# Attention values in half precision by casting transfers of the GpSimd queue, on one core

## The chip, the cores and the metric

The kernel runs on one core of a Trainium2 chip. The metric is the device time of one execution in microseconds (us). A core has five engines that run at the same time, each with a queue of instructions that it takes strictly in order: TensorE (PE, matmuls; PEld are its weight loads), VectorE (DVE), ScalarE (ACT), GpSimd (POOL) and SyncE (SP, which here issues transfers). Transfers between memory and the on-chip buffers run on 16 DMA engines.

## The reference, cut to what matters

A block-causal attention over 8 batches with 8 heads, 576 positions and a head size of 64 (blocks of 64 positions) is followed by a gated linear unit whose gate is a causal convolution over 5 positions.

```python
scores = scale * np.matmul(q, k.transpose(0, 1, 3, 2))       # q, k, v: (8, 8, 576, 64) fp32
scores = np.where(block_i >= block_j, scores, -1e9)
attn = np.exp(scores - scores.max(-1, keepdims=True)); attn /= attn.sum(-1, keepdims=True)
x = np.matmul(attn, v).transpose(0, 2, 1, 3).reshape(8, 576, 512)
gate = sigmoid(sum(conv_w[k] * xp[:, k:k + 576, :] for k in range(5)))
out = (gate * (x @ w_val)) @ w_out                           # fp32
```

## The kernel before

The 64 heads are worked as 32 pairs; pair p is two heads of batch p // 4. The first 512 key positions of a pair are four blocks of 128, the last 64 positions (the tail) are handled per batch. Nothing is left to a scheduler: a text `PLAN` lists words `name/arguments/engine/bank`, and the kernel emits one operation for each word in that order. The order of the words of one engine is the order of that engine's queue. The engine letters are P (TensorE), V (VectorE), A (ScalarE), G (GpSimd) and S (SyncE).

The words that matter here:

- `lq`, `lk` (line 265) load q and k of two pairs, one half each, in fp32 into `qks`; `cd` (line 253) casts them to fp16 on GpSimd or VectorE; `Tt` transposes them on TensorE and `Te` moves the result to `qkT`.
- `S(p, t)` makes the scores of pair p in three parts, `E(p, t)` (line 449, ACT) writes their exponentials to `pts`, six buffers used in turn. `mka` and `mkb` (lines 494 and 499, GpSimd) then zero the masked blocks of `pts`.
- `lv(p, h)` (line 281) loads the values of head h of pair p, 512 rows of 64 fp32 numbers, from SyncE into the staging tiles `vs`, five buffers in turn. `cv(p)` (line 253) casts both heads of pair p from `vs` into `v16s`, seven buffers in turn whose rows are 65 wide: 64 values and a column of ones that `pv` (line 333) writes once. `cv` runs 24 times on GpSimd and 8 times on VectorE.
- `lvt` and `cvt` do the same for the tail, in `vts` and `v16t`.
- `A(p)` on TensorE multiplies the exponentials by `v16s`; the column of ones gives the sums of the softmax. `AT(b)` does it for the tail queries of batch b and reads all four pairs of the batch again. `Nr` and `Nm` (lines 523 and 528, VectorE) normalize, `X` and `Xe` transpose into `xt`.
- `C`, `CS`, `V`, `Ve`, `O`, `Oe`, `Od` are the convolution as matmuls, the gate, the two products and the output. `lcv`, `ccv`, `CW` and `CWe` load, cast, transpose and spread the convolution's weights at the start. `w0` are matmuls on zeros.

The opening (pairs 0 to 3 in halves: `Tth`, `Teh`, `Sh`, `Eh`) comes before the steady part, in which score work of later pairs is mixed with the gated unit of earlier batches. The words after the last attention pair are the output's.

Of the kernel before, what the change touches and what calls it, by code (L numbers as in the profile page):

```python
# [30 lines left out]
E/5.1/A S/6.1/P/6+7 mkb/4/G Nr/2/V AT/0/P/0 Nm/2/V E/6.1/A lk/4.1/S Xe/3/V S/5.0/P/4+5 NTr/0/V
X/2/P/2+3 lv/6.0/S w0/1.128.0/P/1 E/5.0/A Xe/2/V mka/6/G S/7.2/P/6+7 NTm/0/V cwv/1/G S/6.2/P/2+3
E/7.2/A C/0/P/0+1+4+5 lv/6.1/S cwv/0/V E/6.2/A cwo/0/V V/0.3/P/6 CS/0.1/A lq/5.0/S cwo/1/G V/0.2/P/7
CS/0.0/A Ve/0.3/V S/7.1/P/4+5 V/0.0/P/2 Ve/0.2/V E/7.1/A lq/5.1/S cd/4.0/G W//P/0+1+6+7 Ve/0.0/V
lv/5.1/S S/7.0/P/4+5 We/1/A We/0/V V/0.1/P/3 lv/5.0/S mkb/6/G cv/4/G lv/7.1/S E/7.0/A Tt/4.0/P/6+7
Ve/0.1/V lv/7.0/S XT/0/P/2 cd/4.1/G A/4/P/0+1 Te/4.0/A lvt/1/S O/0.0/P/3 Nr/4/V Nm/4/V lk/5.0/S
cv/6/G XTe/0/A SL/1/P/6+7 Oe/0.0/V Tt/4.1/P/4+5 mka/5/G lq/6.0/S EL/1/A mka/7/G A/6/P/0+1 mkb/7/G
Te/4.1/A mkb/5/G O/0.2/P/6 lk/5.1/S cd/5.0/V lq/6.1/S Nr/6/V Tt/5.0/P/4+5 Nm/6/V Oe/0.2/A X/4/P/4+5
lv/8.0/S S/9.2/P/2+3 cv/5/G Te/5.0/V S/8.2/P/6+7 E/9.2/A A/5/P/0+1 E/8.2/A Xe/4/V lv/9.1/S
S/8.0/P/2+3 Nr/5/V cv/7/V S/9.0/P/4+5 lv/8.1/S E/8.0/A cvt/1/G Nm/5/V A/7/P/6+7 lv/10.0/S E/9.0/A  # L40
S/9.1/P/0+1 lv/9.0/S Nr/7/V AT/1/P/2 Nm/7/V lv/10.1/S E/9.1/A S/8.1/P/4+5 lk/6.1/S X/5/P/6+7
cd/5.1/G X/7/P/6+7 X/6/P/6+7 O/0.1/P/3 E/8.1/A Xe/7/V lk/6.0/S Xe/6/V mkb/9/G Xe/5/V Tt/5.1/P/0+1
cd/6.0/G Oe/0.1/A NTr/1/V C/1/P/4+5+6+7 NTm/1/V Te/5.1/A mkb/8/G lv/11.1/S mka/8/G Tt/6.0/P/2+3
CS/1.0/A Od/0.0/S V/1.2/P/0 cv/8/V lv/11.0/S Te/6.0/V CS/1.1/A lk/7.1/S S/11.1/P/4+5 V/1.0/P/1
cv/9/G lvt/2/S E/11.1/A Ve/1.2/V cv/10/G lq/7.1/S S/10.0/P/2+3 Ve/1.0/V A/8/P/6+7 mka/9/G E/10.0/A
lk/7.0/S S/10.2/P/0+1 Nr/8/V S/10.1/P/4+5 lq/7.0/S Nm/8/V E/10.2/A V/1.1/P/2 lv/12.1/S cd/6.1/V
E/10.1/A S/11.2/P/6+7 lv/14.0/S Ve/1.1/V S/11.0/P/0+1 V/1.3/P/3 lvt/3/S E/11.2/A cv/11/V mkb/10/G
A/9/P/4+5 mka/10/G Ve/1.3/V E/11.0/A mkb/11/G Tt/6.1/P/6+7 Nr/9/V A/10/P/2+3 Nm/9/V Te/6.1/A
# [36 lines left out]
E/22.2/A Od/1.2/S S/23.1/P/4+5 Ve/5.1/V lv/26.0/S Tt/12.0/P/0+1 E/23.1/A S/23.2/P/6+7 mkb/22/G
# [34 lines left out]
def kernel(  # L120
# [123 lines left out]
    def rot(tiles, i):  # L244
        return tiles[i % len(tiles)]
# [519 lines left out]
```

## Time and profile before

| what | value |
|---|---|
| time, median of 2 runs | 179.12 us (178.89 to 179.35) |
| the profiled execution | 177.31 us, span 175.5 us |
| PE busy | 165.6 us, 94% |
| ACT busy | 144.8 us, 82% |
| DVE busy | 121.6 us, 69% |
| POOL busy | 70.9 us, 40% |
| transfers | 40.38 MB, 53,694 packets |
| mean granted TensorE clock | 0.968 |

The span runs from the first to the last instruction of the profiled execution; the time around it is that of the whole execution. A busy share is an average over stages that have different limits: an engine with 40% can still be the one that others wait for in a stage. Each group of instructions is named by its line, engine, operation and tiles; a helper such as the copy at line 253 stands for several words of the plan, which the tile names tell apart.

### The profile page before, as it was taken

How to read it: one execution, taken by the hardware profiler on the slowest of the kernel's cores; microseconds unless marked ns; L12 is line 12 of the kernel's file. 1: busy time of each engine (PE TensorE's matmuls, PEld its weight loads, DVE VectorE, ACT ScalarE, POOL GpSimd, SP SyncE). 2: the span in 40 equal slices, each digit the busy share in tenths (PEclk: the TensorE clock that was granted, in tenths of full speed). 3: DMA queues.
4: the chain of work that ended last, by engine and by line, in shares of the span. 5: the costliest groups of instructions: out<-in, count | busy, mean ns of one | idle time of the engine just before them, and what ended most of it. 6: DMA issues, size and time to landing. Idle time of an engine off the chain costs nothing.

```text
span 175.5 us, 8114 instructions
## 1 busy us (share of the span) xinstructions
PE 165.6 (94%) x3498; PEld 99.6 (57%) x3498; DVE 121.6 (69%) x247; ACT 144.8 (82%) x179; POOL 70.9 (40%) x146
## 2 busy tenths in 40 slices
PE   6799899899999899899999999999999999999991
PEld 1456566456756465567556755665556665664540
DVE  2547998588769683999756998976698685545420
ACT  3799999889999699789889679988898878954562
POOL 5121875772552631486533643174546440100000
PEclk9855999999999999999999999999999999999998
DMA  4999899999999779998999969999987022103175
GB/s 141 306 364 280 234 241 392 327 232 252 238 301 262 132 185 287 334 292 241 311 327 246 304 197 259 290 302 222 322 253 213 4 97 86 63 4 120 38 296 209
DMA packets 53694, 40.38 MB, mean 230 GB/s; under 512 B 39701, under 2 KB 39957, under 8 KB 53658
## 3 DMA queue, kind: packets, MB, share of 16 engines
q1 hardware_dynamic: 53514, 39.74, 78.7%
q8 instruction: 27, 0.44, 1.1%
q10 hardware_dynamic: 144, 0.13, 0.2%
q14 instruction: 9, 0.07, 0.1%
HBM read 30.42 MB, written 9.44 MB: 227 GB/s over the span
## 4 chain that ended last, share of the span: by engine, by line
PE 80%; ACT 9%; DVE 3%; issue 3%; DMA 2%; SPq 0%; DVEq 0%; ACTq 0%
PE PS L144 72%; PE PS L148 8%; ACT pt L449 7%; DMA qs<-in_q_dram 2%; DVE gv L658 1%; ACT qkT L251 1%; DVE x L528 1%; DVE qkT L253 1%; DVE xt L253 0%; ACT q L251 0%; SPq L265 0%; ACT osb L251 0%; DVE rc L523 0%; ACT pt L488 0%; ACT late L251 0%
## 5 line engine op out<-in xcount | busy, mean ns | idle before, releaser
L449 ACT ACTIVATE pt<-PS 128x1024 f16<-128x1024 f32 (+1 forms) x102 | 93.8, 988 | 10.4 <-PE PS L144 8.8
L144 PE MATMUL PS<-qkT 64*128 64x64 f16 (+4 forms) x512 | 39.7, 257 | 2.3 <-issue 0.8
L144 PE MATMUL PS<-w_out,gv 128*128 128x512 f16 (+1 forms) x148 | 35.7, 374 | 0.2 <-DVE x L528 0.2
L144 PE MATMUL PS<-xt,w_val 128*128 128x464 f16 x160 | 35.7, 360 | 0.0
L658 DVE SCALAR_TENSOR_TENSOR gv<-th,PS 128x112 f16<-128x112 f32 (+4 forms) x64 | 26.2, 450 | 12.3 <-PE PS L144 6.0
L253 DVE COPY qkT<-PS 128x1152 f16<-128x1152 f16 (+1 forms) x22 | 29.1, 1326 | 8.1 <-PE PS L148 4.0
L144 PEld LDWEIGHTS <-pt 128*128 128x128 f16 (+1 forms) x960 | 27.9, 102 | 6.5 <-issue 1.8
L144 PE MATMUL PS<-v,pt 128*128 128x65 f16 (+1 forms) x896 | 31.1, 194 | 0.2 <-issue 0.2
L144 PEld LDWEIGHTS <-qkT 64*128 64x128 f16 x512 | 17.7, 96 | 18.6 <-issue 14.2
L640 ACT ACTIVATE th<-PS 128x928 f32<-128x928 f32 x20 | 17.8, 941 | 7.2 <-PE PS L144 7.1
L528 DVE TENSOR_TENSOR x<-PS,rc 128x512 f16<-128x512 f32 x32 | 22.1, 691 | 1.0
L144 PEld LDWEIGHTS <-w_val 128*128 128x128 f16 x160 | 13.9, 97 | 15.2 <-issue 3.6
L499 POOL MEMSET pt<- 64x256 f16 x32 | 10.9, 345 | 27.7 <-ACT pt L449 27.3
L144 PEld LDWEIGHTS <-gv 128*128 128x128 f16 x148 | 12.6, 97 | 13.5 <-issue 2.2
L253 POOL CAST k<-ks 128x1152 f16<-128x1152 f32 x12 | 13.8, 1148 | 11.9 <-DMA ks<-in_k_dram 6.0
L253 POOL CAST q<-qs 128x1152 f16<-128x1152 f32 x11 | 12.6, 1147 | 12.9 <-PE PS L144 6.1
L253 POOL CAST v<-vs 128x512 f16<-128x512 f32 x24 | 14.6, 618 | 6.7 <-DMA vs<-in_v_dram 5.1
L494 POOL MEMSET pt<- 64x256 f16 x32 | 10.0, 313 | 17.3 <-ACT pt L449 16.5
L253 DVE COPY xt<-PS 128x512 f16<-128x512 f16 (+1 forms) x30 | 11.6, 397 | 4.5 <-ACT th L640 2.3
L251 ACT COPY qkT<-PS 128x1152 f16<-128x1152 f16 (+1 forms) x16 | 14.2, 908 | 0.4 <-PE PS L148 0.4
L144 PE MATMUL PS<-xt,DG 32*32 32x464 f16 x800 | 13.0, 358 | 0.8 <-issue 0.7
L253 DVE COPY osb<-PS 128x512 f32<-128x512 f32 x17 | 11.6, 687 | 2.4 <-PE PS L144 1.7
(57 smaller groups left out, 135.3 us busy)
## 6 DMA issues: line engine op xcount, KB each, us to landing
ks<-in_k_dram SPq DMA_DIRECT2D x32, 288.0 KB, 5.0
qs<-in_q_dram SPq DMA_DIRECT2D x32, 288.0 KB, 5.5
out_dram<-osb SPq DMA_DIRECT2D x35, 256.0 KB, 4.3
vs<-in_v_dram SPq DMA_DIRECT2D x64, 128.0 KB, 5.1
vts<-in_v_dram SPq DMA_DIRECT2D x8, 128.0 KB, 5.0
osb<-in_moe_w_out_dram SPq DMA_DIRECT2D x2, 512.0 KB, 4.6
gv<-in_moe_w_val_dram SPq DMA_DIRECT2D x2, 512.0 KB, 5.7
out_dram<-late SPq DMA_DIRECT2D x1, 128.0 KB, 2.0
```

The costliest lines, as they stand in the source:

```text
L144: made.append(nc.tensor.matmul(out=out, lhsT=lhsT, rhs=rhs, start=start, stop=stop, skip_group_check=True))
L148: made.append(nc.tensor.transpose(out=out, in_=in_, identity=identity))
L251: i = nc.scalar.copy(out=out, in_=in_)
L253: i = (nc.vector if eng == "V" else nc.gpsimd).tensor_copy(out=out, in_=in_)
L449: made.append(nc.scalar.activation(out=o, in_=r, func=AF.Exp, bias=0.0, scale=0.125))
L494: nc.gpsimd.memset(rot(pts, p)[64:128, 0:2, 0:1024].rearrange("p h (t s) -> p h t s", t=2)[:, :, :, 0:64], 0.0)
L499: nc.gpsimd.memset(rot(pts, p)[64:128, 0:2, 640:1408].rearrange("p h (t s) -> p h t s", t=2)[:, :, :, 0:64], 0.0)
L528: made.append(nc.vector.tensor_tensor(out=rot(x16, p)[0:128].rearrange("p i h d -> p h i d"), in0=r[:, :, :, 0:64], in1=rot(rcs, p)[0:128] ...
L640: made.append(nc.scalar.activation(out=rot(ths, n)[0:128, 2 * i:2 * i + 2], in_=both(take("C", n, i))[:, :, 0:RUN], func=AF.Tanh, bias=0.0 ...
L658: made.append(nc.vector.scalar_tensor_tensor(out=gv[0:128, x, a - 4 * i:e - 4 * i], in0=rot(ths, n)[0:128, x, a - o:e - o], scalar=1.0, in ...
```

## The change

`lv` writes its rows straight into `v16s`, as fp16, and is issued from the GpSimd queue, which casts in the transfer. The staging tiles `vs` and all 32 `cv` are removed. All other words of the plan keep their order.

```diff
-    vs = consts(5, [128, 4, 2, 64], fp32, "vs")
...
-    DMA = {"S": nc.sync, "A": nc.scalar}
+    DMA = {"S": nc.sync, "A": nc.scalar, "G": nc.gpsimd}
...
     def lv(p, h, eng="S", bank=None):
         b, g = divmod(p, 4)
         DMA[eng].dma_start(
-            out=rot(vs, p)[0:128, 0:4, h, 0:64],
+            out=rot(v16s, p)[0:128, 0:4, h, 0:64],
             in_=v[b, 2 * g + h, 0:512, 0:64].rearrange("(c p) d -> p c d", p=128))
...
-    @op
-    def cv(p, eng, bank=None):
-        copy(eng, rot(v16s, p)[0:128, 0:4, 0:2, 0:64], rot(vs, p)[0:128])
```

In `PLAN` the 64 words `lv/p.h/S` and the 32 words `cv/p` are gone. The words `lv/0.0/G lv/0.1/G lv/1.0/G lv/1.1/G` stand between `pv` and `pt` at the start. The other pairs stand two words together, nearly always where a `cv` stood; some of the places, in order:

| pair loaded | stands where | pair loaded | stands where |
|---|---|---|---|
| 2 | `cv/0` | 9 | `cv/7` (VectorE) |
| 3 | `cv/1` | 12 | `cv/10` |
| 5 | `cv/3` | 21 | `cv/19` |
| 4 | `cv/2` | 24 | `cv/22` |
| 6 | `cv/4` | 27 | `cv/25` |
| 8 | `cv/6` | 31 | `cv/29` |
| 7 | `cv/5` | 30 | `cv/28` |

```diff
-E/2.0/A w0/1.128.0/P/4 lv/2.0/S cv/0/G Te/2.0/V S/3.2/P/4+5 E/2.2/A lv/2.1/S Tt/3.0/P/2+3 mkb/1/G
-mka/2/G mkb/0/G lwo/0/S Te/3.0/V E/3.2/A cv/1/G S/3.0/P/6+7 A/0/P/0+1 mka/1/G E/3.0/A S/4.1/P/4+5
+E/2.0/A w0/1.128.0/P/4 lv/2.0/G lv/2.1/G Te/2.0/V S/3.2/P/4+5 E/2.2/A Tt/3.0/P/2+3 mkb/1/G mka/2/G
+mkb/0/G lwo/0/S Te/3.0/V E/3.2/A lv/3.0/G lv/3.1/G S/3.0/P/6+7 A/0/P/0+1 mka/1/G E/3.0/A S/4.1/P/4+5
```

More of the change, by code (lines that the diff above doesn't have):

```diff
@@ L31 @@
[L31 to L48, printed above, removed]
@@ new lines @@
+lv/4.1/G S/6.0/P/0+1 Nr/3/V S/5.1/P/4+5 Nm/3/V cvt/0/G E/6.0/A A/2/P/2+3 px//G Xe/1/V mka/4/G
+X/3/P/2+3 E/5.1/A S/6.1/P/6+7 mkb/4/G Nr/2/V AT/0/P/0 Nm/2/V E/6.1/A lk/4.1/S Xe/3/V S/5.0/P/4+5
+NTr/0/V X/2/P/2+3 w0/1.128.0/P/1 E/5.0/A Xe/2/V mka/6/G S/7.2/P/6+7 NTm/0/V cwv/1/G S/6.2/P/2+3
+E/7.2/A C/0/P/0+1+4+5 cwv/0/V E/6.2/A cwo/0/V V/0.3/P/6 CS/0.1/A lq/5.0/S cwo/1/G V/0.2/P/7 CS/0.0/A
+Ve/0.3/V S/7.1/P/4+5 V/0.0/P/2 Ve/0.2/V E/7.1/A lq/5.1/S cd/4.0/G W//P/0+1+6+7 Ve/0.0/V S/7.0/P/4+5
+We/1/A We/0/V V/0.1/P/3 mkb/6/G lv/6.0/G lv/6.1/G E/7.0/A Tt/4.0/P/6+7 Ve/0.1/V XT/0/P/2 cd/4.1/G
@@ new lines @@
+A/4/P/0+1 Te/4.0/A lvt/1/S O/0.0/P/3 Nr/4/V Nm/4/V lk/5.0/S lv/8.0/G lv/8.1/G XTe/0/A SL/1/P/6+7
+Oe/0.0/V Tt/4.1/P/4+5 mka/5/G lq/6.0/S EL/1/A mka/7/G A/6/P/0+1 mkb/7/G Te/4.1/A mkb/5/G O/0.2/P/6
+lk/5.1/S cd/5.0/V lq/6.1/S Nr/6/V Tt/5.0/P/4+5 Nm/6/V Oe/0.2/A X/4/P/4+5 S/9.2/P/2+3 lv/7.0/G
+lv/7.1/G Te/5.0/V S/8.2/P/6+7 E/9.2/A A/5/P/0+1 E/8.2/A Xe/4/V S/8.0/P/2+3 Nr/5/V lv/9.0/G lv/9.1/G
+S/9.0/P/4+5 E/8.0/A cvt/1/G Nm/5/V A/7/P/6+7 E/9.0/A S/9.1/P/0+1 Nr/7/V AT/1/P/2 Nm/7/V E/9.1/A
+S/8.1/P/4+5 lk/6.1/S X/5/P/6+7 cd/5.1/G X/7/P/6+7 X/6/P/6+7 O/0.1/P/3 E/8.1/A Xe/7/V lk/6.0/S Xe/6/V
@@ new lines @@
+A/10/P/2+3 Nm/9/V Te/6.1/A mka/11/G SL/2/P/0+1 cvt/2/G Nr/10/V A/11/P/4+5 lq/8.0/S Nm/10/V EL/2/A
+X/9/P/4+5 S/12.2/P/6+7 Nr/11/V cd/7.1/G S/12.1/P/0+1 Xe/9/V E/12.2/A O/0.3/P/2 Nm/11/V cd/7.0/G
+E/12.1/A S/12.0/P/4+5 Oe/0.3/V X/8/P/6+7 O/0.5/P/3 lk/8.1/S Xe/8/V E/12.0/A S/13.2/P/6+7 Oe/0.5/V
+Tt/7.0/P/0+1 E/13.2/A mka/12/G lq/8.1/S Tt/7.1/P/4+5 mkb/12/G Te/7.0/V X/10/P/4+5 AT/2/P/3 lv/14.0/G
+lv/14.1/G Te/7.1/A S/13.1/P/6+7 NTr/2/V XT/1/P/2 A/12/P/0+1 NTm/2/V E/13.1/A XTe/1/V Xe/10/V
+X/11/P/0+1 S/14.0/P/2+3 lk/8.0/S lv/16.0/G lv/16.1/G Nr/12/V S/13.0/P/4+5 Xe/11/V E/14.0/A Od/0.2/S
@@ new lines @@
+O/0.6/P/6 mkb/13/G Nm/12/V lq/9.1/S lv/15.0/G lv/15.1/G E/13.0/A lk/9.0/S C/2/P/0+1+2+3 lk/9.1/S
+Oe/0.6/A mka/13/G lq/9.0/S S/14.2/P/4+5 CS/2.0/A V/2.0/P/6 cd/8.0/V CS/2.1/A V/2.2/P/7 Ve/2.0/V
+E/14.2/A Tt/8.0/P/2+3 Ve/2.2/V S/14.1/P/0+1 V/2.1/P/6 E/14.1/A Te/8.0/V Od/0.6/S cd/8.1/G
+S/15.1/P/4+5 A/13/P/0+1 E/15.1/A Ve/2.1/V mka/14/G XT/2/P/7 Nr/13/V Tt/8.1/P/2+3 mkb/14/G lq/10.1/S
+XTe/2/A Nm/13/V X/12/P/2+3 S/15.0/P/4+5 S/15.2/P/6+7 E/15.0/A Te/8.1/V lk/11.0/S O/0.4/P/0 cd/9.1/G
+lq/10.0/S E/15.2/A A/14/P/4+5 cvt/3/G Xe/12/V Od/0.3/S Oe/0.4/V X/13/P/4+5 lv/17.0/G lv/17.1/G
@@ new lines @@
+SL/3/P/2+3 S/16.2/P/6+7 EL/3/A Nr/14/V V/2.3/P/1 mka/15/G Nm/14/V mkb/15/G E/16.2/A cd/9.0/G
+A/15/P/2+3 Ve/2.3/V Xe/13/A S/16.0/P/6+7 Nr/15/V AT/3/P/1 Nm/15/V E/16.0/A S/16.1/P/4+5 NTr/3/V
+lv/21.0/G lv/21.1/G Tt/9.1/P/2+3 lk/11.1/S NTm/3/V E/16.1/A X/15/P/6+7 Tt/9.0/P/6+7 lv/18.0/G
+lv/18.1/G Te/9.1/V Od/0.1/S O/0.8/P/1 Te/9.0/A lk/10.1/S mkb/16/G mka/16/G S/17.2/P/4+5 Oe/0.8/V
+lk/12.1/S A/16/P/2+3 cd/10.0/G E/17.2/A Xe/15/V S/17.0/P/0+1 Nr/16/V S/18.0/P/6+7 Nm/16/V E/17.0/A
+Tt/10.0/P/4+5 lk/10.0/S X/14/P/4+5 XT/3/P/2 Xe/14/V O/1.0/P/3 E/18.0/A Te/10.0/V S/18.1/P/0+1
@@ new lines @@
+XTe/3/A S/17.1/P/6+7 E/18.1/A lq/11.0/S cd/11.1/G O/0.7/P/2 Oe/1.0/V lq/11.1/S E/17.1/A
+C/3/P/0+1+4+5 Oe/0.7/V lv/20.0/G lv/20.1/G mka/17/G C/4/P/2+3+6+7 mkb/17/G CS/3.1/A mka/18/G
+lk/14.1/S Od/0.7/S V/3.2/P/4 lv/19.0/G lv/19.1/G CS/4.1/A V/4.3/P/5 cd/10.1/G CS/4.0/A Ve/3.2/V
+lvt/4/S V/4.1/P/6 Ve/4.3/V CS/3.0/A lvt/5/S S/19.0/P/2+3 Ve/4.1/V S/19.1/P/4+5 V/3.3/P/7 E/19.1/A
+V/4.2/P/6 Od/0.5/S Ve/3.3/V E/19.0/A S/18.2/P/4+5 Ve/4.2/V S/19.2/P/0+1 E/18.2/A X/16/P/2+3 Od/0.4/S
+Tt/10.1/P/2+3 A/17/P/6+7 lq/12.1/S Te/10.1/A mkb/18/G V/4.0/P/4 lk/12.0/S Nr/17/V cd/11.0/G Nm/17/V
@@ new lines @@
+lk/13.0/S V/3.1/P/5 E/19.2/A Ve/4.0/V A/18/P/6+7 Xe/16/V mkb/19/G Ve/3.1/V cvt/4/G SL/4/P/2+3
+S/20.1/P/0+1 Nr/18/V EL/4/A V/3.0/P/5 mka/19/G Nm/18/V E/20.1/A lq/12.0/S A/19/P/2+3 Ve/3.0/V
+S/20.0/P/0+1 Nr/19/V Tt/11.0/P/6+7 lq/14.0/S Nm/19/V E/20.0/A AT/4/P/5 lv/24.0/G lv/24.1/G Te/11.0/V
+S/21.0/P/2+3 X/19/P/0+1 X/17/P/0+1 E/21.0/A O/1.1/P/4 Xe/17/V cd/12.1/G Xe/19/V S/20.2/P/2+3
+Oe/1.1/V S/21.1/P/0+1 E/20.2/A X/18/P/6+7 Tt/11.1/P/6+7 NTr/4/V Od/1.1/S O/1.4/P/4 Te/11.1/V
+lk/15.1/S E/21.1/A mkb/20/G O/1.3/P/2 Od/1.0/S lv/23.0/G lv/23.1/G Oe/1.4/A lq/13.1/S Xe/18/V
@@ new lines @@
+cd/13.0/G V/5.2/P/2 E/23.2/A A/22/P/4+5 Ve/5.2/V X/20/P/4+5 S/24.2/P/0+1 mkb/23/G XTe/4/V Xe/20/A
+S/24.1/P/6+7 O/1.5/P/3 E/24.2/A Nr/22/V cd/13.1/G Nm/22/V lk/14.0/S V/5.3/P/2 E/24.1/A mka/23/G
+X/22/P/4+5 Ve/5.3/V Tt/13.1/P/4+5 X/21/P/0+1 mkb/24/G Tt/13.0/P/0+1 Te/13.1/A Oe/1.5/V S/25.1/P/6+7
+AT/5/P/2 Xe/21/V Od/1.5/S E/25.1/A O/1.6/P/3 lq/14.1/S NTr/5/V lv/26.0/G lv/26.1/G NTm/5/V Xe/22/V
+Te/13.0/A A/23/P/6+7 O/2.2/P/2 lv/28.0/G lv/28.1/G Nr/23/V Oe/1.6/A Nm/23/V Od/1.3/S S/25.0/P/0+1
+S/24.0/P/4+5 E/25.0/A X/23/P/6+7 O/1.8/P/3 Xe/23/V Od/1.6/S cd/14.1/G E/24.0/A C/6/P/0+1+6+7
@@ new lines @@
+Oe/2.2/V mka/24/G Oe/1.8/V Od/2.2/S cd/14.0/G A/24/P/4+5 CS/6.1/A O/2.1/P/3 Od/1.8/S Nr/24/V
+CS/6.0/A Nm/24/V lv/27.0/G lv/27.1/G lq/15.0/S S/26.1/P/6+7 Oe/2.1/V lk/15.0/S Tt/14.0/P/4+5
+E/26.1/A S/25.2/P/0+1 Te/14.0/V O/2.0/P/2 E/25.2/A XT/5/P/3 S/26.2/P/6+7 Oe/2.0/V X/24/P/4+5
+Tt/14.1/P/4+5 E/26.2/A mkb/25/G S/26.0/P/0+1 XTe/5/V Te/14.1/V V/6.0/P/2 Od/2.0/S E/26.0/A mkb/26/G
+V/6.2/P/3 cvt/6/G Ve/6.0/V Od/2.1/S mka/25/G Xe/24/A mka/26/G SL/6/P/0+1 S/27.2/P/6+7 lv/29.0/G
+lv/29.1/G Ve/6.2/V EL/6/A A/25/P/4+5 cd/15.0/G E/27.2/A A/26/P/2+3 Nr/25/V Nm/25/V S/27.1/P/0+1
@@ new lines @@
+S/27.0/P/6+7 Nr/26/V E/27.1/A V/6.3/P/4 Nm/26/V V/6.1/P/5 E/27.0/A mkb/27/G Ve/6.3/V S/28.1/P/0+1
+Ve/6.1/V X/25/P/2+3 mka/27/G Tt/15.0/P/2+3 E/28.1/A S/29.0/P/6+7 Xe/25/V AT/6/P/5 lv/31.0/G
+lv/31.1/G lv/30.0/G lv/30.1/G Te/15.0/V E/29.0/A cd/15.1/G A/27/P/0+1 X/26/P/0+1 NTr/6/V
+S/28.2/P/6+7 NTm/6/V Xe/26/V S/28.0/P/2+3 E/28.2/A Nr/27/V O/2.4/P/5 Nm/27/V E/28.0/A O/2.3/P/4
+Oe/2.4/A S/29.1/P/0+1 mka/28/G Tt/15.1/P/2+3 mkb/28/G E/29.1/A X/27/P/2+3 S/29.2/P/6+7 Te/15.1/V
+O/2.6/P/5 E/29.2/A mka/29/G cvt/7/G A/28/P/0+1 Xe/27/V Oe/2.3/A Oe/2.6/V mkb/29/G C/7/P/2+3+6+7
@@ new lines @@
+Od/2.3/S Od/2.4/S Nr/28/V V/7.3/P/5 Od/2.6/S Nm/28/V CS/7.1/A V/7.1/P/4 CS/7.0/A Ve/7.3/V
+S/30.1/P/6+7 S/30.2/P/0+1 Ve/7.1/V E/30.1/A S/30.0/P/2+3 O/2.5/P/5 E/30.0/A V/7.2/P/4 E/30.2/A
+A/29/P/6+7 Ve/7.2/V S/31.1/P/2+3 Nr/29/V mkb/30/G S/31.2/P/0+1 Nm/29/V mka/30/G V/7.0/P/4 E/31.2/A
+Oe/2.5/V A/30/P/6+7 Ve/7.0/V E/31.1/A Od/2.5/S SL/7/P/0+1 X/29/P/0+1 Nr/30/V X/28/P/0+1 S/31.0/P/4+5
+Nm/30/V mkb/31/G O/3.0/P/2 E/31.0/A O/2.7/P/3 Xe/29/A mka/31/G Xe/28/A A/31/P/4+5 EL/7/A XT/6/P/6
+O/2.8/P/7 Nr/31/V XTe/6/A Nm/31/V X/30/P/0+1 X/31/P/4+5 Xe/30/A AT/7/P/6 Xe/31/V Oe/2.7/A
```

112 lines of the change are left out of this document (31 added, 81 removed).

## The prediction, made before the changed kernel ran

> **What bounds the kernel now.** I read the busy times, the chain and the waits first.
>
> ```profile
> span 175.5 us, 8114 instructions
> PE 165.6 (94%) x3498; PEld 99.6 (57%) x3498; DVE 121.6 (69%) x247; ACT 144.8 (82%) x179; POOL 70.9 (40%) x146
> PE 80%; ACT 9%; DVE 3%; issue 3%; DMA 2%; SPq 0%; DVEq 0%; ACTq 0%
> POOL pt L499 <- ACT pt L449: 27.3, 14, 5.4
> POOL pt L494 <- ACT pt L449: 16.5, 13, 3.4
> ```
>
> TensorE is busy 94% and carries 80% of the chain; no step of POOL is among the chain's engines. All idle time of TensorE is 175.5 - 165.6 = 9.9 us, so work taken off other engines can win little. POOL looks free at 40%, but 43.8 us of its idle time are two memsets that wait for the exponentials: POOL runs in order, and work put ahead of such a memset uses that time only as far as it fits. So the question is what each stage of POOL can take. Two answers of the table by stage show it, POOL whole and then the instructions on the staging tile `vs` alone (columns: stage, width, busy time with count).
>
> ```profile
> 18.00:35.00 17.00, 12.26 (x27) 1.00 1.03 306
> 35.00:50.00 15.00, 8.40 (x16) 1.00 1.03 254
> 50.00:65.00 15.00, 5.95 (x12) 1.00 0.85 205
> 65.00:80.00 15.00, 7.58 (x14) 1.00 1.02 301
> 80.00:95.00 15.00, 5.97 (x11) 1.00 1.02 277
> 95.00:110.00 15.00, 7.42 (x13) 1.00 0.90 257
> 110.00:125.00 15.00, 6.45 (x11) 1.00 1.01 275
> 125.00:142.00 17.00, 9.12 (x18) 1.00 0.56 168
> ...
> 18.00:35.00 17.00, 0.00 (x0) 2.94 (x5) 1.00 1.03 306
> 35.00:50.00 15.00, 0.83 (x2) 2.26 (x5) 1.00 1.03 254
> 50.00:65.00 15.00, 0.43 (x1) 0.90 (x2) 1.00 0.85 205
> 65.00:80.00 15.00, 0.42 (x1) 1.93 (x4) 1.00 1.02 301
> 80.00:95.00 15.00, 0.43 (x1) 1.10 (x2) 1.00 1.02 277
> 95.00:110.00 15.00, 0.84 (x2) 1.24 (x2) 1.00 0.90 257
> 110.00:125.00 15.00, 0.00 (x0) 1.23 (x2) 1.00 1.01 275
> 125.00:142.00 17.00, 0.00 (x0) 2.41 (x4) 1.00 0.56 168
> ```
>
> In the second answer the first pair is DVE, the second POOL. Without the value casts POOL's spare time is, stage by stage, width - (POOL - POOL on `vs`): 7.68, 8.86, 9.95, 9.35, 10.13, 8.82, 9.78, 10.29 us.
>
> **What is removed.** These groups carry it:
>
> ```profile
> L253 POOL CAST v<-vs 128x512 f16<-128x512 f32 x24 | 14.6, 618 | 6.7 <-DMA vs<-in_v_dram 5.1 <-PE PS L144 1.0
> L253 DVE CAST v<-vs 128x512 f16<-128x512 f32 x8 | 3.7, 468 | 1.1 <-DMA vs<-in_v_dram 1.1
> L281 SPq DMA_DIRECT2D vs<-in_v_dram x64: 368/594/2200, 7.8 to 131.3; - x64
> DMA to landing us min/median/max: 3.4/5.1/7.5
> ```
>
> POOL loses 24 casts (14.6 us), DVE 8 (3.7 us), SP 64 issues of 0.594 us median (38 us). None stands on the chain: DVE is 69% busy and SP waits more than it issues. I cost these at no gain on the path; POOL's part is already in the spare times above.
>
> **What is added.** The 64 transfers now go out from POOL, two per pair. In the new plan each `cv` word is replaced, where it stood, by the two `lv` words of another pair, mostly p+2. So a stage gets two transfers for each cast that starts in it, POOL's or DVE's. A cast that starts just before a boundary is counted once (the second stage's five POOL rows hold the tail of one of 34.5 us). The counts are 10, 12, 4, 10, 4, 8, 4, 8; four more (pairs 0 and 1) stand in the opening. The sum is 64.
>
> The price x of one such transfer on POOL has no row. The low bound is SP's 0.594 us median for the same 512 packets of 256 bytes; the high bound is that row's longest issue, 2.20 us. POOL has to produce addresses for 512 rows in software, and the nearest POOL row that goes through 512 items is the 128x512 cast, 618 ns. I take the issue plus such a pass: x = 0.594 + 0.618 = 1.21, rounded to 1.2 us. This choice carries the forecast.
>
> The excess n·x - spare of each stage, where positive, at x = 1.2: 12.0 - 7.68 = 4.32; 14.4 - 8.86 = 5.54; 4.8 - 9.95, none; 12.0 - 9.35 = 2.65; none; 9.6 - 8.82 = 0.78; none; 9.6 - 10.29, none. The sum is 13.3 us. I let it all reach the path, because what is queued behind a late POOL transfer are the memsets `mka`/`mkb` that A(p) needs and the q and k casts that the transposes need, and TensorE takes all of these in a fixed order. TensorE's queue behind A(p) holds the scores, so ACT's exponentials are late next, and with them the memsets again.
>
> Landing does not come on top. The shortest lead is at pair 3, whose transfers stand where this cast stood, ahead of these matmuls:
>
> ```profile
> 20.62 0.62 POOL L253 CAST v<-vs 128x512 f16<-128x512 f32 x1
> L144 PE MATMUL PS<-v,pt x40: 191/193/204, 25.1 to 27.0; 128*128 128x65 f16 x40
> ```
>
> Pair 2's two transfers delay it by 2.4 - 0.62 = 1.8 us; the second transfer goes out 1.2 us later and lands 5.1 us after that: 20.6 + 1.8 + 1.2 + 5.1 = 28.7, against 25.1. That is 3.6 us, within the 4.32 already charged to this stage.
>
> **The opening.** Four transfers are put between the first and the later memsets, ahead of the cast of the convolution's weights.
>
> ```profile
> 1.25 0.35 POOL L333 MEMSET v<- 128x8 f16 x7
> 2.03 0.98 POOL L347 MEMSET vts<- 64x512 f32 x2
> 4.87 0.60 POOL L253 CAST conv<-late 5x512 f16<-5x512 f32 x1 [1.86 <-DMA late<-in_moe_conv_w_dram]
> 5.88 0.25 PE L144 MATMUL PS<-ident,conv 5*128 5x5 f16 x4
> 6.06 0.39 PE L144 MATMUL PS<-th 128*128 128x512 f16 x1
> 7.08 1.23 PE L144 MATMUL PS<-qkT 64*128 64x320 f16 x7 [0.63 <-ACT qkT L251]
> ```
>
> The first memsets end at 1.60, the others take until 3.01, that is 1.4 us. The cast then begins at 1.6 + 4x + 1.4, ends 0.6 later, and the four matmuls on `conv`, a filler and the first scores follow in TensorE's order: 5.88 to 6.45 is 0.57 us. So the first scores start at 4.2 + 4x, or at 7.08 if that is later. At x = 1.2 it is 9.0: 1.9 us, with nothing to hide it, since the chain runs through these scores. Their break-even is x = 0.72.
>
> **Waits that the new order brings.** A buffer of the seven is now refilled two pairs earlier, so the transfer waits for `A` and `AT` of pair p-7. In the trace most of these readers are done long before; the worst place is pair 24, issued where a cast started at 98.23 and waiting for AT(4):
>
> ```profile
> 98.23 0.62 POOL L253 CAST v<-vs 128x512 f16<-128x512 f32 x1
> 100.30 0.20 PE L144 MATMUL PS<-v16t,pt 128*64 128x65 f16 x2
> ```
>
> POOL would stand there for 100.50 - 98.23 = 2.3 us, with a memset behind it. The stage before has 10.13 - 4.8 = 5.3 us to spare and the lead to A(24) is long, so I count nothing; without that cover it is 2.3 us, within the range. POOL's later transfers also wait for the one eight before them, long landed.
>
> A rule of the Trainium skill speaks against the change: "SBUF — State Buffer", section "SBUF: two separate sides", says that a transfer from the GpSimd queue cannot have its descriptors written while VectorE runs a copy in a two-port mode.
>
> ```profile
> L253 DVE CAST q<-qs 128x1152 f16<-128x1152 f32 x4 | 3.4, 860 | 3.0 <-issue 3.0
> L253 DVE CAST k<-ks 128x1152 f16<-128x1152 f32 x3 | 2.2, 732 | 0.0
> ```
>
> By that rule the large VectorE casts left that read SBUF would block POOL by at most 3.4 + 2.2 = 5.6 us, and the sum would be up to 5.6 us higher, some 200 us; no row shows it, and I leave it out.
>
> **Sum.** 13.3 + 1.9 = 15.2 us. The profiled execution took 177.31 us around its span of 175.5 and would take 192.5. The median of the two runs shown is 179.12, 1.8 above it; there the sum gives 194.3.
>
> **Rivals.** (1) *POOL's issue costs about what SP's does.* Below x = 0.74 (8.86/12) no stage overflows and below 0.72 the opening keeps its time. At 0.594 the stages need 5.9 of 7.68 and 7.1 of 8.86. Left is landing at pair 3: 20.6 + 0.6 + 0.6 + 5.1 = 26.9 against 25.1, or 1.8 us: 181 us, not slower by what can be told. For it: SP's issue time does not depend on the row count, and POOL's idle 43.8 us. Against: POOL has no row with so short a step for so many addresses. The Trainium skill leans this way ("DMA: Bandwidth & Descriptors", section "Anatomy of one DMA — SWDGE (gpsimd) path": making the descriptors is a small part, and many can be made before it shows); no run here shows it. (2) *POOL becomes the bound in most stages*, x near 2.2: 14.3 + 17.5 + 12.7 + 8.8 + 7.3 = 60.6, opening 13.0 - 7.08 = 5.9: 179.1 + 66.5 = 246 us. For it: 64 x 512 = 32,768 rows handled in software. (3) *The transfers themselves get dearer.* DMA is at 1.01 to 1.03 of its engines' time in five stages, so a dearer casting packet has no cover there.
>
> ```profile
> DMA packets 53694, 40.38 MB, mean 230 GB/s; under 512 B 39701, under 2 KB 39957, under 8 KB 53658
> q1 hardware_dynamic: 53514, 39.74, 78.7%
> ```
>
> By bytes (8.4 of 39.7 MB) values take 0.21 x 138 = 29 us of the queue's 138; if their packets took twice as long, 29 us would be added: 208 us. Against: the same bytes are read and half are written. (4) *Faster*: SP's free time brings q and k earlier and DVE loses 3.7 us; it ends at 175, since even all of DVE's 3% of the chain is 5 us and POOL's load speaks against it.
>
> **Chances.** Forecast, x from 0.9 to 1.6: 0.50. At 0.9 the sum is 1.32 + 1.94 + 0.7 = 4.0, at 1.6 it is 8.3 + 10.3 + 6.7 + 4.0 + 2.5 + 3.5 = 35.3: its own range is 183 to 214. Rival 1: 0.16. Rival 2 and what lies between it and 1.6: 0.25. Rival 3: 0.06. Rival 4: 0.03. A measurement can tell 2%, 3.6 us. Faster is rival 4, within 2% is rival 1, the rest is slower: 0.03, 0.16, 0.81. The range reaches down to rival 1 without its stall, 179, and up to x = 2.0 (12.3 + 15.1 + 10.7 + 7.2 + 5.7 + 5.1 = 56), 235.
>
> **What would show it.** Right: POOL's step per transfer near 1.2 us; the first scores near 9 us; the matmuls on v and the weight loads of pt waiting for POOL and for the values between 20 and 50 us; later stages with little spare time on POOL. Wrong: POOL's gaps below 0.75 us and an unchanged TensorE, or long packets on the casting queue with a short step on POOL.

## The result, and the profile after

The changed kernel takes 198.59 us (median of 2 runs, 198.55 to 198.63) against 179.12 us: a ratio of 1.109 with a 95% interval of 1.103 to 1.115, slower by about 11%. A second set of runs on another chip gave 1.099 (1.092 to 1.106). The kernel before differs by a per cent or so between chips, so every ratio below is to the kernel before on the same chip. Executions of one kernel fall into a faster and a slower group; the times below are medians of all runs while the ratios compare the faster groups, so that two times need not give the ratio beside them, and the profile of e_pairs32 is of a slower run.

The page of the changed kernel first: the span, the busy times, two of the DMA queues, the chain by engine and by line.

```profile
span 196.7 us, 8090 instructions
PE 172.0 (87%) x3498; PEld 102.4 (52%) x3498; DVE 119.8 (61%) x239; ACT 145.5 (74%) x179; POOL 104.0 (53%) x186
DMA packets 53692, 36.17 MB, mean 184 GB/s; under 512 B 39701, under 2 KB 39957, under 8 KB 53658
q1 hardware_dynamic: 19722, 31.34, 49.5%
q0 software_dynamic: 33792, 4.20, 34.0%
PE 58%; DMA 19%; POOL 12%; issue 5%; DVE 2%; ACT 1%; SPq 1%; POOLq 0%; ACTq 0%
L278 POOL DMA_DIRECT2D v<-in_v_dram x64 | 48.8, 774 | 5.4 <-PE PS L142 4.8
```

The span of the profiled execution grew by 21.2 us (the medians differ by 19.5). TensorE's idle time went from 9.9 to 196.7 - 172.0 = 24.7 us, and its busy time from 165.6 to 172.0 for the same 3,498 matmuls. POOL's share rose to 53%, with 64 transfers at a mean of 774 ns. What is new on the chain are DMA, 19% after 2%, and POOL, 12% where it had no share. The waits and the rows of the tile `v` (what the instruction is, its min/median/max in ns, and the time from issue to landing) name the first:

```profile
PE PS L142 <- DMA v<-in_v_dram: 14.4, 5, 7.4
POOL v L278 <- PE PS L142: 4.8, 4, 2.1
PEld L142 <- POOL pt L487: 2.0, 3, 1.6
...
L278 POOL DMA_DIRECT2D v<-in_v_dram x64: 740/750/1082, 1.6 to 159.0; - x64
DMA to landing us min/median/max: 2.5/4.6/15.3
```

TensorE waits 14.4 us, in five waits, for values that have not landed. In the kernel before this wait does not exist. The median landing, 4.6 us, is even shorter than the 5.1 us of before; the longest is 15.3 us, after 7.5. The timeline of TensorE (start, us, what, idle time before it and what ended it) shows the place, and the timeline of POOL when the transfers were issued:

```profile
33.87 0.71 PE L142 MATMUL PS<-v,pt 128*128 128x65 f16 x10 [7.44 <-DMA v<-in_v_dram]
37.00 0.71 PE L142 MATMUL PS<-v,pt 128*128 128x65 f16 x10 [2.42 <-DMA v<-in_v_dram]
38.61 1.28 PE L142 MATMUL PS<-v,pt 128*128 128x65 f16 x20
...
18.99 1.82 POOL L278 DMA_DIRECT2D v<-in_v_dram  x2
21.56 1.49 POOL L278 DMA_DIRECT2D v<-in_v_dram  x2
41.82 0.31 POOL L487 MEMSET pt<- 64x256 f16 x1 [12.01 <-ACT pt L442]
```

The transfers of pair 2 go out at 18.99, those of pair 3 at 21.56, the second of these at about 22.3. Pair 3 is needed at about 26.4 (33.87 less the wait of 7.44). Its first head is there at 33.87, its second at 37.00. The chain in order of time has this as one piece, and a second such piece late in the kernel, at pair 22, where TensorE waited 2.41 us:

```profile
22.29 14.67 DMA v<-in_v_dram
...
124.28 9.48 DMA v<-in_v_dram
...
133.80 0.71 PE L142 MATMUL PS<-v,pt 128*128 128x65 f16 x10 [2.41 <-DMA v<-in_v_dram]
```

The matmuls on v of pair 2 began at 26.41 in the kernel before (the row below) and begin at 38.61 now. So 12.2 of the 21.2 us are lost by then. Behind the stall everything in TensorE's order is late: the memset on `pt` at 41.82 waited 12.01 us for its exponentials.

```profile
26.41 0.78 PE L144 MATMUL PS<-v,pt 128*128 128x65 f16 x20
```

The table by stage of the changed kernel (width, then PE, PEld, DVE, ACT and POOL busy, the granted clock, DMA share, GB/s) shows a second loss at the same place:

```profile
24.00:30.00 6.00, 2.35 (x66) 1.73 (x63) 2.98 (x5) 3.60 (x4) 5.67 (x16) 1.00 1.23 329
30.00:34.00 4.00, 0.13 (x3) 0.13 (x3) 0.00 (x0) 0.00 (x0) 0.00 (x0) 0.63 1.47 243
34.00:38.00 4.00, 1.57 (x22) 1.14 (x22) 0.20 (x1) 0.00 (x0) 0.00 (x0) 0.50 1.22 334
38.00:42.00 4.00, 4.00 (x88) 2.89 (x84) 2.44 (x7) 2.96 (x3) 0.18 (x1) 0.59 0.70 73
```

Between 30 and 34 us VectorE, ScalarE and GpSimd do nothing and TensorE only 0.13 us; transfers run. When the values arrive, TensorE runs on at a granted clock of 0.50 to 0.59, so that the 20 matmuls of pair 2 take 1.28 us where they took 0.78. This loss is not all net: the profiled execution of the kernel before has a stretch at about half clock too, in its opening, where the changed kernel has none. The pages' rows of the granted clock, in tenths for 40 equal slices of the span, before and then after:

```profile
PEclk9855999999999999999999999999999999999998
PEclk9999996589997999999999999996999999999998
```

### The profile page after: what moved, and what is told of

The parts are those of the page before. It is cut to its first block, busy times and chain, and to the rows that moved or that the text cites. A ratio compares the mean times of both kernels' runs of the same rounds, so it can differ in the third digit from the quotient of the medians.

```text
span 196.7 us, 8090 instructions
## 1 busy us (share of the span) xinstructions
PE 172.0 (87%) x3498; PEld 102.4 (52%) x3498; DVE 119.8 (61%) x239; ACT 145.5 (74%) x179; POOL 104.0 (53%) x186
## 3 DMA queue, kind: packets, MB, share of 16 engines
q1 hardware_dynamic: 19722, 31.34, 49.5%
q0 software_dynamic: 33792, 4.20, 34.0%
HBM read 30.42 MB, written 9.44 MB: 203 GB/s over the span
## 4 chain that ended last, share of the span: by engine, by line
PE 58%; DMA 19%; POOL 12%; issue 5%; DVE 2%; ACT 1%; SPq 1%; POOLq 0%; ACTq 0%
PE PS L142 53%; DMA v<-in_v_dram 15%; POOL v L278 6%; PE PS L146 5%; DMA out_dram<-osb 3%; POOL pt L487 1%; POOL q L250 1%; POOL k L250 1%; POOL pt L492 1%; ACT pt L442 1%; ACT osb L248 1%; SPq L262 1%; DVE xt L250 1%; POOL v16t L250 1%; DVE qkT L250 1%
## 5 line engine op out<-in xcount | busy, mean ns | idle before, releaser
L278 POOL DMA_DIRECT2D v<-in_v_dram x64 | 48.8, 774 | 5.4 <-PE PS L142 4.8
L142 PE MATMUL PS<-v,pt 128*128 128x65 f16 (+1 forms) x896 | 33.6, 200 | 15.9 <-DMA v<-in_v_dram 14.4
L142 PE MATMUL PS<-qkT 64*128 64x64 f16 (+4 forms) x512 | 42.3, 267 | 1.8 <-DVE rc L516 0.7
L142 PEld LDWEIGHTS <-pt 128*128 128x128 f16 (+1 forms) x960 | 30.1, 107 | 23.1 <-issue 16.5
L142 PE MATMUL PS<-w_out,gv 128*128 128x512 f16 (+1 forms) x148 | 36.3, 379 | 0.0
L492 POOL MEMSET pt<- 64x256 f16 x32 | 9.9, 311 | 27.9 <-ACT pt L442 27.6
L516 DVE RECIPROCAL rc<-PS 128x8 f32<-128x8 f32 x32 | 6.6, 205 | 26.7 <-issue 10.7
L487 POOL MEMSET pt<- 64x256 f16 x32 | 9.9, 314 | 22.9 <-ACT pt L442 22.3
L142 PEld LDWEIGHTS <-w_val 128*128 128x128 f16 x160 | 14.0, 98 | 15.3 <-issue 3.8
L250 POOL CAST q<-qs 128x1152 f16<-128x1152 f32 x11 | 13.2, 1200 | 11.3 <-DMA qs<-in_q_dram 4.8
L248 ACT COPY osb<-PS 128x512 f32<-128x512 f32 x18 | 10.5, 591 | 3.7 <-PE PS L142 3.5
```

The lines of the kernel that those rows point to most:

```text
L142: made.append(nc.tensor.matmul(out=out, lhsT=lhsT, rhs=rhs, start=start, stop=stop, skip_group_check=True))
L248: i = nc.scalar.copy(out=out, in_=in_)
L250: i = (nc.vector if eng == "V" else nc.gpsimd).tensor_copy(out=out, in_=in_)
L278: DMA[eng].dma_start(out=rot(v16s, p)[0:128, 0:4, h, 0:64], in_=v[b, 2 * g + h, 0:512, 0:64].rearrange("(c p) d -> p c d", p=128))
L487: nc.gpsimd.memset(rot(pts, p)[64:128, 0:2, 0:1024].rearrange("p h (t s) -> p h t s", t=2)[:, :, :, 0:64], 0.0)
L492: nc.gpsimd.memset(rot(pts, p)[64:128, 0:2, 640:1408].rearrange("p h (t s) -> p h t s", t=2)[:, :, :, 0:64], 0.0)
```

## The experiments

Two theories stood against each other. The landing theory: the casting transfers take turns with the loads of q and k, packet by packet, and land late, and where the lead is short TensorE waits. The POOL theory: the time and the issuing of 64 transfers on POOL delay its memsets and casts, whatever the transfers carry.

The packet records of the trace (counted over all queues) say what the casting transfers are. With the cast, each row of 64 values is a packet of its own: 32,768 packets of 128 bytes for the values, 32.3 ns each. Their number is not new: the kernel before sent the same rows in as many packets, of 256 bytes and 19.8 ns each, but in SP's queue, in line with q and k. Between 27 and 29 us and between 34 and 38 us some 150 value packets start in each us, and beside them some 136 of q's and k's, which carry 2,304 bytes: about one for one. At that rate 512 rows take 512/150 = 3.4 us and four transfers in a row some 14 us, about the time from the first packet of pair 2, at 23.5 us, to the landing of pair 3's second transfer, at 36.96. Where few or no loads of q and k are under way, some 500 to 900 value packets start in a us. The Trainium skill has the rule for it ("DMA: Bandwidth & Descriptors", section "Queues, rings and completion order"): each DMA engine goes round the queues that have work for it, one packet at a time. The counts agree. They do not explain the start: the first packet of pair 2 starts 4.5 us after its issue at 18.99, while other transfers fill the engines, where 1.5 us pass after the issue at 46.54, with the engines idle. No run takes these 3 us apart.

### e_pairs32: only pairs 3 and 2 earlier

```diff
  ccv//G
+ lv/3.0/G lv/3.1/G lv/2.0/G lv/2.1/G
  ...
- lv/2.0/G lv/2.1/G    (where cv/0 stood)
- lv/3.0/G lv/3.1/G    (where cv/1 stood)
```

> The changed kernel with one edit: the casting transfers of pairs 3 and 2 are issued right after the cast of the convolution's weights (near 7 us) instead of at 19 and 21.6 us. Theory A (late landing: the casting queue shares the DMA engines packet by packet with the bulk loads, and the leads of some 5 us are too short): the 10.9 us that A(3) and A(2) lost go, and the time is 187 to 189 us. Theory B (POOL's own 49 us of issue is what is paid): the same work stands on POOL, 197 to 199 us. Theory C (a casting packet of 128 bytes costs the engines 32 ns where a plain one cost less, and the engines are the bound): 197 to 199 us.

Measured: 188.77 us against 177.43 us, a ratio of 1.053 (1.044 to 1.062); span 188.1 us. The wait and the rows of TensorE that answer to those above:

```profile
PE PS L142 <- DMA v<-in_v_dram: 3.9, 3, 1.9
...
28.05 0.78 PE L142 MATMUL PS<-v,pt 128*128 128x65 f16 x20
```

Pair 2 is late by 1.6 us instead of 12.2, the wait for values falls from 14.4 to 3.9 us, and about half of the loss is gone with the move of four words. The transfers do not land faster for it, the longest now 16.2 us after its issue; they are issued earlier. The number of packets, their bytes and the work of POOL are as in the changed kernel: its casting queue takes 35.4% of 188.1 us, 66.6 us of the engines' time, and took 34.0% of 196.7, 66.9 us. So this half comes from single transfers that land after they are needed. It is not the DMA engines' total time, which did not change.

### e_quiet: less beside the transfers

```diff
- lq/4.0/S lq/4.1/S lk/4.0/S lk/4.1/S
- lq/5.0/S lq/5.1/S lk/5.0/S lk/5.1/S
```

> The changed kernel without the eight loads of q and k of pairs 8 to 11 (the casts then read what an earlier load left, so these pairs' scores are not the reference's). These loads run from 24 to 38 us beside the values of pairs 2 and 3, which landed 15 us after their issue. Theory A, in its form of taking turns: a cast row is a packet of its own and takes a turn against one bulk packet of 2304 bytes, so without the bulk the second transfer of pair 3 lands before 30 us instead of 37, and A(2) starts at 29 to 32 us instead of 38.6; of the 12 us lost there 6 to 9 come back. If the casting queue is slow by itself (its packets, its descriptors), it lands at 35 us or later.

Measured: 193.45 against 178.51 us, 1.084 (1.075 to 1.092), with the changed kernel at 1.099 on the same chip. The landing and the two pairs:

```profile
DMA to landing us min/median/max: 2.7/4.9/11.1
...
32.36 1.48 PE L141 MATMUL PS<-v,pt 128*128 128x65 f16 x20 [6.18 <-DMA v<-in_v_dram]
34.74 1.28 PE L141 MATMUL PS<-v,pt 128*128 128x65 f16 x20
```

With four pairs' loads of q and k gone, the longest landing falls from 15.3 to 11.1 us and pair 2 begins 3.9 us earlier. That is the right direction and less than the 6 to 9 us that the landing theory wanted: the second transfer of pair 3 landed at 33.1 us, between the 30 of that theory and the 35 or later of a queue that is slow by itself. What was left beside the transfers until about 32 us, by the packet records, were the weights' loads and the other loads of q and k; after that the value packets ran alone, 730 in the next us. The first packet of pair 2 again started 4.5 us after its issue. So the neighbours bear on the landing, but the experiment did not take all of them away.

### e_nocast: the same queue without the cast

```diff
+ lv/0.0/G lv/0.1/G lv/1.0/G ...        (fp32, on the GpSimd queue, into vs)
- lv/0.1/S lv/0.0/S lv/1.1/S ...
-     vs = consts(5, [128, 4, 2, 64], fp32, "vs")
+     vs = consts(8, [128, 4, 2, 64], fp32, "vs")
```

All `cv` stay, each transfer stands two casts ahead of its own.

> The kernel before with the value loads moved to the GpSimd queue, two pairs ahead of the cast that reads them, but in fp32 into eight staging tiles; the casts stay on GpSimd and VectorE. It tells the queue from the cast. Theory A: the loads land as late as in the changed kernel (up to 10 us and more after issue between 20 and 40 us), POOL has its casts besides, and the time is 197 to 210 us; packets of 256 bytes on the GpSimd queue cost about as much as they do now. Theory C (the cast makes the packet dear): the mean packet falls from 32 ns to about 20 ns and the time to 185 to 192 us. Theory B: POOL carries 49 + 15 us, 203 to 212 us.

Measured: 191.68 against 177.43 us, 1.077 (1.068 to 1.085). Its GpSimd queue, the group of its transfers, the landing of the values, then of q and of k, and a wait of POOL:

```profile
q0 software_dynamic: 3072, 8.39, 16.4%
...
L282 POOL DMA_DIRECT2D vs<-in_v_dram x64 | 48.8, 768 | 0.4 <-DVE gv L659 0.2
...
DMA to landing us min/median/max: 2.7/5.2/7.7
DMA to landing us min/median/max: 3.1/6.2/14.1
DMA to landing us min/median/max: 3.2/6.4/14.7
...
POOL q L254 <- DMA qs<-in_q_dram: 12.2, 3, 5.9
```

The same 512 rows per transfer go as packets of 4,096 bytes, 16 rows in one: 2,048 packets for the values where the cast made 32,768. There are few of them, and no landing of values exceeds 7.7 us, though they carry twice the written bytes. So the landing theory missed here: it had wanted values as late as in the changed kernel. The queue alone does not make them late; the queue with a packet for every row does. (The written tile differs too, fp32 rows in `vs`, so the cast is not the only difference.) POOL's price is the same with the cast and without it, 774 and 768 ns.

What costs the time here is not settled. TensorE waits for the casts, as in the kernel before, and on POOL these wait only 2.2 us for values. But q and k land after up to 14.1 and 14.7 us, where the kernel before has 7.9 and 8.0, and POOL waits 12.2 us for q. POOL also makes 64 transfers and still does 24 casts, 119.5 us in all, and weight loads wait 6.4 us for one group of its memsets. Nor does this run by itself rule out that the packets are merely dearer: its time lies in the range of that theory, and its queue took 16.4% of 189.0 = 31.0 us of the engines' time where the casting queue took 66.9. The Trainium skill ("DMA: Bandwidth & Descriptors", section "Rules for kernel authors") sends a cast in the transfer to GpSimd; in this case's trace that came with one row in a packet.

### e_busy34 and e_busy: POOL's time without transfers

```diff
+ nc.gpsimd.memset(spare[0:128, 0:520], 0.0)    (e_busy34; 0:740 in e_busy)
+ bz//G bz//G   at each of the places of the changed kernel, 64 in all; all else as before
```

> The kernel before with 64 memsets of 0.53 us of a spare tile on POOL, two at each place where the changed kernel has its two transfers, no transfer added. It adds 34 us to POOL, what the changed kernel adds net of its removed casts (48.8 - 14.6). If POOL's time is what the added short transfers cost: 1.03 to 1.05. If that was their traffic: 1.00 to 1.015.

> The kernel before with 64 memsets of 0.76 us of a spare tile on POOL, two at each place where the changed kernel has its two transfers, and no transfer added: POOL's time alone, 49 us on top of 71. Theory B (POOL's time, paid where memsets and casts stand behind it): more than the 1.040 of the added short transfers of 0.55 us, 1.05 to 1.09. If that 1.040 came from the traffic or the descriptors and not from POOL's time: 1.00 to 1.015.

Measured: e_busy34 (536 ns each, 34 us in all) 1.006 (1.001 to 1.010), e_busy (720 ns each, 46 us) 1.060 (1.047 to 1.074). POOL is busy 106.1 and 118.0 us; the changed kernel's POOL has 104.0. So POOL of the changed kernel is as full as in e_busy34, which loses half a per cent, and POOL's plain time can't explain the rest. The step from 106 to 118 us is steep: 12 us more of POOL cost some 5 points, with 7.1 us of weight loads waiting for memsets in the row below (e_busy).

```profile
PEld L148 <- POOL pt L503: 7.1, 8, 1.8
```

### e_issue and e_issue16: short transfers without use

```diff
+ nc.gpsimd.dma_start(out=spare[i % 8][0:128, 0:64], in_=v[i // 8, i % 8, 0:128, 0:64])   (0:16 in e_issue16)
+ ld/0/G ld/1/G ...   64 at the same places; all else as before
```

> The kernel before with 64 short transfers of 128 rows added on the GpSimd queue, at the places where the changed kernel has its casting transfers; nothing reads what they bring, and the value loads stay on SyncE. It tells what POOL's issue time alone costs. If the price per transfer is the same as for 512 rows (0.75 us), POOL gets 48 us on top of its 71. Theory A: 179 to 182 us. Theory B: 190 us or more. Theory C: 179 to 182 us.

> The kernel before with 64 transfers of only 16 rows (4 KB each) added on the GpSimd queue at the places where the changed kernel has its casting transfers. The transfers of 128 rows cost 1.040, memsets of the same 34 us on POOL 1.006. If what the 128 rows cost was their traffic on the engines (7 us of all 16 engines) or their landing beside q and k: 1.00 to 1.015 now. If it was the making of descriptors on POOL whatever the rows (0.48 us each, worked out from 0.553 us at 128 rows and 0.77 us at 512): 1.025 to 1.04.

Measured: e_issue 1.040 (1.031 to 1.049), its median of 186.35 us between what the two theories had wanted, and e_issue16 1.028 (1.020 to 1.036). The rows of the transfers, e_issue first:

```profile
L293 POOL DMA_DIRECT2D spare<-in_v_dram x64: 534/534/979, 1.7 to 144.1; - x64
```

```profile
L293 POOL DMA_DIRECT2D spare<-in_v_dram x64: 484/484/1067, 1.7 to 143.4; - x64
q0 software_dynamic: 2048, 0.27, 1.0%
```

A transfer of 16 rows takes POOL 484 ns, one of 128 rows 534 ns and one of 512 rows 750 ns: some 0.48 us and half a ns for each row. The two kernels spend 35.1 and 32.2 us of POOL on this, which as memsets cost 0.6%, and lose 4.0% and 2.8%. Making a transfer costs the kernel more than its time on POOL, and in e_issue16 the traffic is 0.27 MB and 1.0% of the engines' time. Why is not settled. The page of e_issue16 has DMA at 17% of the chain (values and the outputs), where the kernel before has 2%; but e_busy34, which loses only 0.6%, has 11%, and the values of e_issue16 land after a median of 4.9 us, no later than before. No run here takes the cause apart.

### e_lead4, e_lead2, e_lead2_open: more lead for all

```diff
-    v16s = consts(7, [128, 4, 2, 65], fp16, "v16")
+    v16s = consts(9, [128, 4, 2, 65], fp16, "v16")     (11 in e_lead4)
  ccv//G
+ lv/3.0/G lv/3.1/G lv/2.0/G lv/2.1/G
  ...
- lv/2.0/G lv/2.1/G
+ lv/4.0/G lv/4.1/G          every later pair two places earlier (e_lead4: four)
```

e_lead2_open also puts `lv/0.*` and `lv/1.*` behind `ccv` instead of ahead of it.

> The changed kernel with eleven value buffers in place of seven, and every casting transfer four pairs earlier (pairs 3 and 2 after the cast of the convolution's weights, 4 and 6 after the first q cast of GpSimd, the others at the places of pairs needed four later). The number of transfers, their size and their price on POOL stay. Theory A: 180 to 184 us, what is left being the opening's 1 us and POOL's delays. Theory B: 195 to 199 us. Theory C: 194 to 199 us.

> The changed kernel with nine value buffers, pairs 3 and 2 loaded after the cast of the convolution's weights, and all later pairs two pairs earlier than in the changed kernel. The first four pairs are the only values in the opening. Theory A (short leads against late landing make all but the cost that the added short transfers showed): TensorE no longer waits for a value transfer, A(4) is 2 to 3 us later than before and the end 6 to 8 us; the ratio to before is 1.035 to 1.045 (185 to 187 us where before takes 179.1). Theory C (the dearer packet keeps the engines busy whatever the lead): 1.06 to 1.08, with q and k landing late.

> As the run with nine buffers and two pairs more lead, and the four transfers of pairs 0 and 1 are also behind the cast of the convolution's weights. If the first scores are late because that cast stands behind four transfers on POOL, they start at 7.1 us again and the time is 0.7 to 1.3 us less than that run's. If it is the transfers' share of the DMA engines in the opening, nothing is won.

Measured: e_lead4 1.076 (1.069 to 1.083), a miss, since the landing theory had wanted 180 to 184 us and the median is 191.2; e_lead2 1.053 (1.038 to 1.068), above the 1.035 to 1.045 that the theory had wanted; e_lead2_open 1.085 (1.071 to 1.098), a loss against e_lead2 where a small gain or none was expected. In e_lead4 and e_lead2 no wait of TensorE on values is left; but e_lead2 is no faster than e_pairs32. Rows of e_lead4, the waits, then the landing of its values:

```profile
PE PS L142 <- POOL pt L487: 5.9, 4, 3.4
PEld L142 <- POOL pt L487: 7.1, 5, 3.5
POOL v L278 <- DMA v<-in_v_dram: 7.6, 5, 2.6
...
DMA to landing us min/median/max: 2.5/7.7/21.4
```

More transfers are in flight at once, and the queue of values and the loads of q and k delay each other. Values land after up to 21.4 us, POOL waits for its own earlier transfers (the third row), its memsets stand behind that, and TensorE waits for memsets. The loads of q and k are late as well. In e_lead2 those of q land after a median of 6.7 us where the kernel before has 5.5, the first row of e_lead2 and the second of before:

```profile
DMA to landing us min/median/max: 3.0/6.7/10.7
```

```profile
DMA to landing us min/median/max: 3.3/5.5/7.9
```

The changed kernel itself has 6.6 for q, and 6.6 for k where the kernel before has 5.0. So this delay came with the change, and more lead did not take it away.

e_lead2_open shows the same in the opening: eight casting transfers behind one another while q and k are loaded. Its first scores start only 0.4 us later than before, so the opening's place on POOL is well mended, but its chain has one piece of 22.13 us on the values:

```profile
11.20 22.13 DMA v<-in_v_dram
```

So in these runs more lead moved the late landing to another place. The casting queue has the same 33,792 packets wherever the transfers stand.

### e_spq: without GpSimd and without casts

```diff
-            in_=v[b, 2 * g + h, 0:512, 0:64].rearrange("(c p) d -> p c d", p=128))
+            in_=flat[0:128].rearrange("p (c d) -> p c d", c=4))
- lv/p.h/G ...      + lv/p.h/S at the places of the kernel before; no cv
```

> The changed kernel with nine value buffers, the value transfers on SyncE at the places of the kernel before, in fp16 and without a cast: they copy an on-chip tile of ones, so the values are left out. It has what the change removes (32 casts, the fp32 staging) and nothing of what it adds on POOL. If the removed casts were worth something: 174 to 176 us where before takes 179.1 (ratio 0.97 to 0.985). If they were hidden: 0.99 to 1.005.

Measured: 178.21 against 178.17 us, 1.006 (1.000 to 1.012); POOL 55.1 us, 31%. All 32 casts and the staging tiles are gone from POOL and VectorE, and nothing is won: the interval reaches down to no change. The run even reads less from memory, 22.03 MB where the kernel before reads 30.42, since the values are left out. What the change removes was hidden.

## Why the prediction was right, and where its steps were not

*That it gets slower, and by how much.* The sum gave 194.3 us and 198.59 was measured, slower as forecast and inside the range. That the number came so close is luck: the largest term of the sum came out small, and a term that the text had set at nothing took its place.

*The price on POOL.* The step x = 1.2 us, an issue plus a pass as long as a cast, was mis-sized: 0.774 us in the mean, 0.750 in the median. By the prediction's own formulas, x = 0.774 gives 10x - 7.68 = 0.06, 12x - 8.86 = 0.43 and nothing in the later stages, and for the opening 4.2 + 4x - 7.08 = 0.22. The sum of 0.7 us is 180 us and not 194.3. The four transfers of the opening took 3.17 us (the first row), the first scores began at 7.78 and not at 9.0:

```profile
1.62 3.17 POOL L278 DMA_DIRECT2D v<-in_v_dram  x4
...
7.78 1.46 PE L142 MATMUL PS<-qkT 64*128 64x320 f16 x7
```

The mechanism was right for the opening: 0.7 us by the row (7.78 less 7.08), if more than the 0.2 of the formula. For the stages, the sums of busy time and spare time would have found almost nothing. e_busy34 says that this is so for plain time, and e_issue and e_issue16 that 64 transfers cost 2.8% to 4.0% all the same. So of the 13.3 us charged to POOL 5 to 7 may be there, but not as plain time on POOL.

*"Landing does not come on top."* This step failed. It used 5.1 us from issue to landing, a median of a single queue in which values stand in line with q and k. On a queue of their own, taking turns with q and k, the same 512 packets of a transfer landed after up to 15.3 us in a row of eight transfers. The prediction had 28.7 us for pair 3 against 25.1; it got its second head at 37.00. e_pairs32 gave back about half of the loss, 8 to 10 us, with the move of two pairs. The place was named right, as the shortest lead.

*Rival 3, dearer transfers (208 us, chance 0.06).* Its price came true, though not by its working: the values cost not 29 us of engine time in the kernel before but 32,768 x 19.8 ns / 16 = 41 us, and 32,768 x 32.3 ns / 16 = 66 us now, and the queues' time together rose from 138 to (49.5% + 34.0%) of 196.7 = 164 us, by 26 where the rival had 29. "The same bytes are read and half are written" was no protection: a packet of 128 bytes written took 32.3 ns, where the packets of 256 bytes took 19.8 ns on SP's queue. But the loss is not this sum alone, as e_pairs32 shows with the same engine time in 9 us less. What part of the rest it makes no run shows. What the prediction named as a sign of being wrong, long packets on the casting queue with a short step on POOL, is what the trace has.

*Rival 1 (POOL's issue at SP's price, 181 us).* Right in its premise: 0.750 us stands near SP's 0.594. The Trainium skill's leaning that was weighed with it ("DMA: Bandwidth & Descriptors", section "Anatomy of one DMA — SWDGE (gpsimd) path"), that making descriptors is a small part, fits the rows in so far as 512 rows cost 0.27 us more than 16. Its conclusion, that then only 1.8 us are lost, fell with the landing.

*The port between VectorE and GpSimd's transfers.* Left out of the sum, at most 5.6 us. The 64 transfers have a minimum of 740 ns and a mean of 774 ns, so all their delays together are at most 64 x 0.034 = 2.2 us. POOL's rows bear out no block of weight.

*The wait at a buffer.* Costed at nothing, with 2.3 us as its price at pair 24. Measured are 4.8 us in four waits of POOL for TensorE, 2.1 the longest, in a kernel whose TensorE is late itself. Its effect by itself was not tried.

*The removed casts.* At no gain: confirmed by e_spq. Rival 4 (faster) has nothing left to stand on. Rival 2 fell with x.

*What stays open.* Why transfers cost more than their time on POOL; how the remaining 5.3% of e_pairs32 divide between that, the late landings that are left (3.9 us of waits), the later landing of q and k and the engines' longer time; why the first packet of pair 2 starts so late. The single losses were measured in different kernels and need not add.

## What to carry to other kernels

Before a load moves to a second queue, ask into how many packets it falls and what takes turns with them: here every row stayed a packet of its own, and in a burst of such loads beside other loads landings took up to 3.3 times their median (15.3 against 4.6 us). The lead that sufficed in one shared queue need not suffice in a second; take the shortest lead in the order and hold it against a burst, not against a median. And ask first whether what goes was on the path: these 32 casts were hidden, and without them nothing was won.

## What the runs showed of the hardware

- The GpSimd queue merged 16 rows of 256 bytes into one packet of 4,096 bytes without the cast and made one packet of 128 bytes per row with it: 2,048 against 32,768 packets, at about the same time on POOL (768 and 774 ns). SP's queue, without a cast, made one packet of 256 bytes per row.
- A transfer of the GpSimd queue takes POOL about 0.48 us and some 0.5 ns for a row (484, 534 and 750 ns at 16, 128 and 512 rows).
- In the changed kernel two queues shared the DMA engines about one packet for one packet, although one's were 18 times as large: some 150 of 128 bytes and 136 of 2,304 bytes started in the same us.
- After a wait of 7 us TensorE's granted clock was 0.50 to 0.59, and 20 matmuls took 1.28 us and not 0.78. In e_pairs32, without that wait, the same matmuls took 0.78 us.
- 64 transfers of 16 rows cost 2.8% where memsets that keep POOL busy as long cost 0.6%.
